# Linear attention before two feed-forward layers: attention by whole load groups, tail products over 128 rows, rms_g folded into the weights, the token scale on ScalarE

## The chip, the cores and the metric

One core of a Trainium2 chip. Its engines are named as in the profile: PE (TensorE matmuls; PEld is its weight load), DVE (VectorE), ACT (ScalarE), POOL (GpSimd) and SP (SyncE, which only issues DMAs). Each engine works through its own instructions in order. The metric is the device time of one execution in microseconds; lower is better.

## The reference

```python
def attn(q, k, v, omega):                 # 4 batches, 8 heads, 576 rows, D = 64, M = 128 features
    def phi(x):                           # x already scaled by D ** -0.25
        h = x @ omega.T - sum(x * x) / 2
        return exp(h - max(h)) / sqrt(M)
    kv, z = phi(k).T @ v, sum(phi(k))     # per batch and head
    return (phi(q) @ kv) / (phi(q) @ z + 1e-6)
def moe(x, w_gate, w_val, w_out, rms_g):  # 2304 tokens, 512 -> 1536 -> 512
    xn = x / sqrt(mean(x * x) + 1e-6) * rms_g
    return (silu(xn @ w_gate) * (xn @ w_val)) @ w_out
def moe2(x, w_in, w_out):                 # 512 -> 2048 -> 512
    return silu(x @ w_in) @ w_out
out = moe2(moe(tokens(attn(...))))        # inputs and weights come as float32 or float64
```

The weights come as float64 and are decoded on the chip. Every product with a weight is done in three passes (high by high, high by low, low by high).

## The kernel before, in words

**Attention and the first sweep.** The 576 rows of a batch are two halves of 256 rows and a tail of 64. One load (`add_load`) brings a half of four heads as a 128x512 tile; the tails of two batches share a tile of 128x256, the even batch in the first 64 partitions and the odd one in the last. A *unit* (`add_unit`) is half a load of a half, or a whole tail: 72 units, 36 of k and 36 of q. For each unit PE transposes 2 blocks (L586), ACT copies them out as the high part (L592), DVE subtracts for the low part (L595), PE does six 256-column products with omega (`pj`, L605), DVE takes the maxima (L620) and forms the bias in two small instructions (L626, L633) from the row norms (squared and halved on POOL, L545 and L549, ended on DVE, L558), and ACT does four exponentials (L644). A unit of k then adds its products with v into one PSUM bank (`kv`, L690); these have 128 rows and two output halves of 64 columns, while a tail of k has 64 rows and a full output. When a batch and four heads are done, DVE copies that bank out (`kvs`, L710). A unit of q is transposed on PE (L721), copied out by ACT (L727) and multiplied by kvs (L736, L742); DVE divides (L759 to L779).

When the heads of a half are complete, ACT squares and sums its tokens (L803), POOL makes rstd (L814, L817), DVE multiplies by rstd and rms_g (`xn`, L833), PE transposes (L842), and ACT and DVE write the high and low part of the tokens (L851, L856) into `xs`. There are 18 such tiles of 128 tokens in five blocks: four of 512 columns and one of 256.

**Weights.** A job (`w_load`, `w_decode`, `w_high`, `w_low`) loads 512 KB, decodes it with five DVE passes (L156 to L167) and two POOL passes (L170), and splits it on ACT (L180) and DVE (L183). Six jobs of the first sweep (two gates, two values, two outputs) and the first three of the second are put between the attention work (`add_weight`); each of the six waits for a numbered `pj`.

**Order.** All this, and the first sweep's products for blocks 0 to 2 (L236, L963), are `Op`s with a duration, dependences and buffer claims. `run_order` walks a model of the five engines and emits at each step the ready Op with the smallest `prio + RANK[kind]`; so the tables `RANK` and `SLOTS`, the durations and the Ops themselves set the order of every engine. Six PSUM banks (`b`) go round among transposes, projections and products.

**The stream.** After that the remaining products (blocks 3 and 4 of sweep 0, then ten more sweeps, five of them in all with gates and values) follow in a written order, and `Prep.tick` puts in a step of the weight pipe whenever PE has been given 3.2 us of work (until the second sweep's weights are in), later 5.5 us. The first product of the stream is the first `PE g L236`.

Of the kernel before, what the change touches and what calls it, by code (L numbers as in the profile page):

```python
# [20 lines left out]
def kernel(  # L21
# [68 lines left out]
    g_sb = const.tile([P, DM], F32)  # L90
# [60 lines left out]
    def w_decode(job, st, step, n=None):  # L151
# [36 lines left out]
    class Prep:  # L188
# [35 lines left out]
    W_EARLY, GRAIN = 3, 3  # L224
# [152 lines left out]
    class Op:  # L377
# [15 lines left out]
        "ld_om": 41.7, "t_om": -211.5, "s_om": -232.3, "bd_hi": -107.5, "bd_lo": 58.9,  # L393
# [4 lines left out]
        "rstd": -389.4, "xn": 36.2, "xf": -367.8, "x_hi": -48.8, "x_lo": 225.6, "ld_w": 11.5,  # L398
        "w_dec": 310.2, "w_add": 254.1, "w_hi": 67.9, "w_lo": 196.9, "part": 226.4, "tanh": 300.8,
        "silu": -31.9, "glu": 10.3, "h_hi": -176.1, "h_lo": -143.8, "out": 711.2, "ya": -190.5,  # L400
    }
    SLOTS = {
# [68 lines left out]
    small = ps_a.tile([P, SLOTS["nb"], 2 * G], F32, tag="small", name="small", bufs=1)  # L471
# [3 lines left out]
    def fetch(dst, src, kind, b, hf, g):  # L475
        heads = slice(G * g, G * g + G)
        if len(kind) == 2:
            for e in range(2):
# [18 lines left out]
    def k_units(b):  # L497
        for g in range(2):
            for hf in range(2):
                for hp in range(2 * g, 2 * g + 2):  # L500
                    yield "k", b, hf, hp, g
            if b % 2 == 0:
                yield "kt", b, 0, 0, g

    def q_units(b):
        for hf in range(2):
            for hp in range(4):
                yield "q", b, hf, hp, hp // 2
# [11 lines left out]
    last_use = {}  # L520
    for i, (kind, b, hf, hp, g) in enumerate(units):
        last_use[kind, b, hf, g] = i
    last_k = max(i for i, u in enumerate(units) if u[0][0] == "k")
# [5 lines left out]
    def add_load(u, i):  # L529
# [9 lines left out]
        w.op = Op("ld_x", "SP", 0.37 * R, emit, prio=i - 5, claim=["x"])  # L539
# [13 lines left out]
        w.sqop = Op("sq", "Pool", 0.26 + 0.43 * R, squares, [w.op], i - 1, ["sq", "ns"])  # L553
        h1 = Op("half1", "Pool", 0.25 + 0.28 * R, lambda o: halve(D // 2), [w.sqop], i - 2)
        h2 = Op("half2", "Pool", 0.26 + 0.14 * R, lambda o: halve(D // 4), [h1], i - 2)
# [6 lines left out]
        w.nsop = Op("norms", "DVE", 0.2, norms, [h2], i + 0.5, free=[(w.sqop, "sq")])  # L562
        if kind[0] == "k":
            z = vld[u] = State()

            def emit_v(o):
                z.v = va_tail[g] if tail else va_ring[o.slot["v"]]
                fetch(z.v, v, *u)

            z.op = Op("ld_v", "SP", 0.73 * R, emit_v, prio=i, claim=[f"vt{g}" if tail else "v"])  # L570

    def add_unit(i):
        kind, b, hf, hp, g = units[i]
        u = kind, b, hf, g
        tail = len(kind) == 2
        if u not in ld:
            add_load(u, i)
        w = ld[u]
        st = State()

        def transposes(o):
            st.pt = buf(ps_a, [P, 2, P], "b", o.slot["b"])
            st.hl = buf(wk, [P, 2, 2, P], "hl", o.slot["hl"], F32R)
            for j in range(2):
                h0, n = (2 * j, 2) if tail else (2 * (hp % 2) + j, 1)
                nc.tensor.transpose(  # L586
                    st.pt[:, j, :], w.x[:, h0:h0 + n, :, :].rearrange("p h r d -> p (h r d)"), ident
                )

        free_x = [(w.op, "x")] if last_use[u] == i else []  # L590
        tr = Op("tr", "PE", 0.218, transposes, [w.op, w.sqop], i - 1, ["b", "hl"], free_x)
        hi = Op("tr_hi", "ACT", 0.264, lambda o: nc.scalar.activation(out=st.hl[:, 0], in_=st.pt, func=AF.Copy), [tr], i - 0.3)  # L592
        lo = Op(
            "tr_lo", "DVE", 0.335,
            lambda o: nc.vector.tensor_tensor(  # L595
                out=st.hl[:, 1], in0=st.pt, in1=st.hl[:, 0].bitcast(F32), op=ALU.subtract
            ),
            [hi], i, free=[(tr, "b")],
        )

        def project(o):
            st.ps = buf(ps_a, [P, G, P], "b", o.slot["b"])
            for j in range(2):
                for n, (a, c) in enumerate(PASS):
                    nc.tensor.matmul(  # L605
# [478 lines left out]
```

## Time and profile before

| | us |
|---|---|
| median of 3 runs (1009.81 to 1011.66) | 1011.57 |
| the profiled execution's own time | 1011.63 |
| its span, first to last instruction | 1009.8 |
| PE busy in the span | 992.4 (98%) |
| first `PE g L236` of the stream | 218.18 |

The page gives for each engine the time in which an instruction ran on it. PE counts as busy while a matmul is in its pipe, and the ends of matmuls are modelled; so PE at 98% says that it nearly always had something in the pipe, not that it ran at its highest rate. The distance from the start of one group to the start of the next, where nothing is waited for, gives the rate. The other engines are read in the same way: the busy time of one instruction includes some latency that the next one overlaps.

### The profile page before, as it was taken

The page shows a single profiled execution, that of the slowest core. Times are in us where ns is not written, and L with a number is a line of the kernel's source. Part 1 is how long each engine was busy: PE and PEld are TensorE (multiplying, and loading weights), DVE is VectorE, ACT ScalarE, POOL GpSimd, SP SyncE. Part 2 cuts the span into 40 slices and gives each one's busy share as a digit, 9 for nine tenths or more (in the row PEclk, how much of TensorE's full clock was granted, in tenths as well). Part 3 has the DMA queues.
Part 4 walks back from the last instruction along what each step waited for, and adds up shares of the span by engine and source line. Part 5 has one row for each costly group of instructions (what it writes and reads, how often), then busy time and mean ns, then how long its engine had stood idle before and what let it go on. Part 6 is the DMA issues. An engine that isn't in the chain of part 4 may idle for free.

```text
span 1009.8 us, 15330 instructions
## 1 busy us (share of the span) xinstructions
PE 992.4 (98%) x5935; PEld 842.4 (83%) x5935; DVE 587.8 (58%) x1289; ACT 374.6 (37%) x861; POOL 282.2 (28%) x287
## 2 busy tenths in 40 slices
PE   7999998999999999999999999999999999999998
PEld 7988886788888888888888888888888888888887
DVE  7899998837852345676332776443654544535633
ACT  6988895344221112222111334433322322322321
POOL 6756632415520002344000231321411411201300
PEclk9999999999999999999999999999999999999999
DMA  7444211212320002222000120210210210200023
GB/s 196 123 122 131 67 30 42 64 41 84 104 63 1 1 1 64 63 85 83 21 1 1 42 63 22 84 42 5 79 42 6 78 42 22 63 1 21 21 84 105
DMA packets 68729, 55.85 MB, mean 55 GB/s; under 512 B 25648, under 2 KB 62768, under 8 KB 68656
## 3 DMA queue, kind: packets, MB, share of 16 engines
q1 hardware_dynamic: 68656, 54.87, 18.4%
q8 instruction: 47, 0.77, 0.3%
q14 instruction: 26, 0.21, 0.1%
HBM read 50.14 MB, written 4.72 MB: 54 GB/s over the span
## 4 chain that ended last, share of the span: by engine, by line
PE 89%; DVE 7%; issue 1%; POOL 1%; ACT 1%; DMA 1%; SPq 0%; DVEq 0%; ACTq 0%; POOLq 0%
PE g L236 43%; PE y L323 19%; PE y L290 12%; PE b L605 4%; PE b L236 3%; PE kv L690 2%; DVE small L620 2%; PE b L963 2%; PE b L736 1%; PE b L721 1%; PE b L586 1%; DVE hl L595 1%; DVE w L183 1%; POOL m L170 1%; DVE xt L833 1%
## 5 line engine op out<-in xcount | busy, mean ns | idle before, releaser
L236 PE MATMUL g<-xs,w 128*128 128x512 f32 (+1 forms) x2256 | 467.9, 366 | 0.0
L236 PEld LDWEIGHTS g<-xs,w 128*128 128x128 f32 x2256 | 391.2, 188 | 70.1
L170 POOL TENSOR_TENSOR m<-m,raw 128x512 int32<-128x512 int32 x136 | 189.9, 1396 | 612.6 <-issue 442.6
L230 DVE TENSOR_TENSOR h<-s,h 128x512 fp32r<-128x512 f32 (+1 forms) x134 | 96.0, 717 | 185.0 <-ACT h L229 185.0
L323 PE MATMUL y<-w,h 128*128 128x512 f32 (+1 forms) x870 | 200.8, 388 | 0.0
L323 PEld LDWEIGHTS y<-w,h 128*128 128x128 f32 x870 | 162.2, 188 | 33.3
L229 ACT ACTIVATE h<-s 128x512 fp32r<-128x512 f32 (+1 forms) x134 | 78.7, 588 | 191.5 <-DVE s L259 169.5
L290 PE MATMUL y<-h,w 128*128 128x512 f32 (+1 forms) x648 | 135.6, 366 | 0.3 <-DVE w L183 0.3
L290 PEld LDWEIGHTS y<-h,w 128*128 128x128 f32 x648 | 112.1, 189 | 20.5 <-DVE w L183 0.8
L270 ACT ACTIVATE s<-g 128x512 f32<-128x512 f32 (+1 forms) x80 | 44.4, 556 | 171.0 <-PE g L236 170.9
L334 DVE TENSOR_TENSOR ya<-y,ya 128x512 f32<-128x512 f32 (+1 forms) x91 | 62.2, 684 | 57.8 <-PE y L323 56.5
L259 DVE TENSOR_TENSOR s<-s,g 128x512 f32<-128x512 f32 (+1 forms) x54 | 33.8, 627 | 84.8 <-PE g L236 84.8
L301 DVE TENSOR_TENSOR ya<-y,ya 128x512 f32<-128x512 f32 (+1 forms) x80 | 50.2, 635 | 54.3 <-PE y L290 54.1
L180 ACT ACTIVATE w<-m 128x512 fp32r<-128x512 f32 x68 | 42.7, 628 | 102.8 <-POOL m L170 102.8
L644 ACT ACTIVATE e<-b,nb 128x128 f32<-128x128 f32 x272 | 77.5, 395 | 3.7 <-DVE nb L633 3.6
L605 PE MATMUL b<-bd,hl 128*128 128x256 f32 x432 | 69.5, 300 | 1.7 <-DVE hl L595 1.1
L605 PEld LDWEIGHTS b<-bd,hl 128*128 128x128 f32 x432 | 56.8, 192 | 5.4 <-DVE hl L595 2.3
L620 DVE TENSOR_REDUCE small<-b 128x4 f32<-128x512 f32 x72 | 50.2, 697 | 6.2 <-PE b L605 2.2
L253 ACT ACTIVATE s<-g 128x512 f32<-128x512 f32 (+1 forms) x54 | 29.7, 550 | 64.1 <-PE g L236 63.9
L183 DVE TENSOR_TENSOR w<-m,w 128x512 fp32r<-128x512 f32 x68 | 52.9, 779 | 0.1
L545 POOL TENSOR_TENSOR sq<-x 128x512 f32<-128x512 f32 (+1 forms) x40 | 38.9, 982 | 36.2 <-DMA x<-in_q_dram 9.8
L549 POOL TENSOR_TENSOR sq<-sq 128x256 f32<-128x256 f32 (+2 forms) x80 | 44.4, 573 | 2.3
(69 smaller groups left out, 739.7 us busy)
## 6 DMA issues: line engine op xcount, KB each, us to landing
raw<-in_moe_w_out_dram SPq DMA_DIRECT2D x28, 512.0 KB, 3.5
raw<-in_moe_w_in_dram SPq DMA_DIRECT2D x16, 512.0 KB, 3.7
raw<-in_moe_w_gate_dram SPq DMA_DIRECT2D x12, 512.0 KB, 3.6
raw<-in_moe_w_val_dram SPq DMA_DIRECT2D x12, 512.0 KB, 3.5
x<-in_k_dram SPq DMA_DIRECT2D x16, 256.0 KB, 3.4
va<-in_v_dram SPq DMA_DIRECT2D x32, 128.0 KB, 3.3
x<-in_q_dram SPq DMA_DIRECT2D x16, 256.0 KB, 3.0
out_dram<-ya SPq DMA_DIRECT2D x15, 256.0 KB, 2.0
```

The source lines that it names most:

```text
L170: tt(out=mi, in0=mi, in1=(low if step == 5 else high).bitcast(I32), op=ALU.add)
L183: nc.vector.tensor_tensor(out=st.t[:, 1, :], in0=st.m.bitcast(F32), in1=st.t[:, 0, :].bitcast(F32), op=ALU.subtract)
L229: nc.scalar.activation(out=ht[:, 0, :], in_=s, func=AF.Copy)
L230: nc.vector.tensor_tensor(out=ht[:, 1, :], in0=s, in1=ht[:, 0, :].bitcast(F32), op=ALU.subtract)
L236: nc.tensor.matmul(out=ps, lhsT=w[:, a, cc * P:(cc + 1) * P], rhs=xs[j][:, c, cc, :], start=(n == 0), stop=(n == 3 * KC - 1),)
L290: nc.tensor.matmul(out=ps, lhsT=wt[1, "o", f][:, a, d * P:(d + 1) * P], rhs=hs[f][:, c, :], start=(n == 0), stop=(n == nn - 1),)
L301: nc.vector.tensor_tensor(out=y[:, d, :], in0=ps, in1=y[:, d, :], op=ALU.add)
L323: nc.tensor.matmul(out=ps, lhsT=hs[f][:, a, t * P:(t + 1) * P], rhs=wt[2, "p", f][:, c, d0:d1], start=(n == 0), stop=(n == nn - 1),)
L334: nc.vector.tensor_tensor(out=o[:, t, d0:d1], in0=ps, in1=o[:, t, d0:d1], op=ALU.add)
L605: nc.tensor.matmul(out=st.ps[:, 2 * j:2 * j + 2, :].rearrange("p h m -> p (h m)"), lhsT=st.hl[:, c, j, :], rhs=bd[:, a, :], start=(n == 0) ...
L620: nc.vector.tensor_reduce(out=st.mx, in_=st.ps, axis=AX.X, op=ALU.max)
L644: nc.scalar.activation(out=st.e[:, h, :], in_=st.ps[:, h, :], func=AF.Exp, bias=st.nb[:, h:h + 1])
```

## The change

- A unit is now a whole load: one transpose group of four blocks, one high and one low copy of 128x512, then two projections, two maxima, one pair of the small bias instructions over 8 columns instead of 4, two groups of exponentials. A load of k ends in one `kv` group of 16 products.
- A tail's `v` tile is padded with zeros in the other batch's 64 partitions, and its products run over 128 rows with two output halves like the others. The tile is filled twice, once for each batch: POOL writes zeros and ones (`pad`), SP loads 64 rows (`ld_vt`). The second `pad` waits for the first batch's products.
- rms_g is loaded as 128x4 and multiplied into the gate and value weights by a third POOL pass (L173). The tokens are then scaled by rstd alone, on ACT (`xn`), and kvs is copied out by ACT as well. The sum of squares writes its unused output into `xs` instead of a buffer of its own.
- The first sweep's weight jobs wait for the `pj` of loads 3, 4, 5, ... instead of units 24, 26, 28, ...
- `RANK` has new values and separate ones for k and q, `SLOTS` has other counts (x 4, hl 2, e 4, nmc 2), several durations of the model are other, and `EDGE` is 72.

```diff
-        else:
+        elif step < 7:
             mi = st.m.bitcast(I32)
             tt(out=mi, in0=mi, in1=(low if step == 5 else high).bitcast(I32), op=ALU.add)
+        else:
+            mf = st.m.bitcast(F32).rearrange("p (c f) -> p c f", c=KC)
+            tt(out=mf, in0=mf, in1=g_sb.rearrange("p (c o) -> p c o", o=1).to_broadcast([P, KC, P]), op=ALU.mult)
+    def scaled(job):
+        return job[2][1] in "gv"
...
-                    for s in range(7):
+                    for s in range(8 if scaled(job) else 7):
...
-        "ev": -296.8, "num": -288, "den": -624.4, "rec": 84.2, "mu": 166, "ss": 2186.9,
+        "ev": -25.5, "num": -251.5, "den": 269.3, "rec": 818.1, "mu": 56.7, "ss": 1947.1,
...
+    def add_tail_v(u, i, e, prev):
+        kind, b, hf, g = u
+        t = va_tail[g]
+        def pad(o):
+            nc.gpsimd.memset(t[64 - 64 * e:P - 64 * e], 0.0)
+            nc.gpsimd.memset(t[64 * e:64 * e + 64, :, :, D:D + 1], 1.0)
+        po = Op("pad", "Pool", 0.35, pad, [prev], i - 2, [] if prev else [f"vt{g}"])
+        return po, Op("ld_vt", "SP", 0.36, lambda o: fetch(t, v, kind, b, hf, g, [e]), [po], i)
...
-            st.pt = buf(ps_a, [P, 2, P], "b", o.slot["b"])
-            st.hl = buf(wk, [P, 2, 2, P], "hl", o.slot["hl"], F32R)
+            st.pt = buf(ps_a, [P, 2 * R, P], "b", o.slot["b"])
+            st.hl = buf(wk, [P, 2, 4, P], "hl", o.slot["hl"], F32R)
+            for j in range(2 * R):
+                nc.tensor.transpose(st.pt[:, j, :], flat()[:, j * P:(j + 1) * P], ident)
...
+        for r in range(R):
+            def project(o, r=r):
...
-                    jobs.append((a, st.e[0:64, a, :], va.v[0:64, a, 0, :]))
+            return [(h, st.e[0][:, h, :], va_tail[g][:, h, 0, :]) for h in range(G)]
...
-                nc.vector.tensor_copy(out=acc.sb, in_=acc.ps)
+                nc.scalar.activation(out=acc.sb, in_=acc.ps, func=AF.Copy)
...
-            nc.vector.scalar_tensor_tensor(
-                out=st.x, in0=st.x, scalar=xs_.rstd[:, r:r + 1], in1=g_sb, op0=ALU.mult, op1=ALU.mult
-            )
-        xn = Op("xn", "DVE", 0.61, scale_x, [rs, g_op], i, free=[(xs_.sq[0], "rs")] if last else [], port=True)
+            nc.scalar.activation(out=st.x, in_=st.x, func=AF.Copy, scale=xs_.rstd[:, r:r + 1])
+        xn = Op("xn", "ACT", 0.53, scale_x, [rs], i, free=[(xs_.sq[0], "rs")] if last else [])
...
-            add_weight(job, n, [pj_ops[24 + 2 * n]])
+            add_weight(job, n, [pj_ops[GATE + n]])
```

How instructions move, in three places. In the names, b is a PSUM bank, hl the split transposes, e the exponentials, xt the tokens, w a weight of side and slot, xs the blocks of tokens; the number behind a name tells buffers apart.

PE before, from the last two projections (L605) to the first product of the stage with a weight (L236):

```order
L605 MATMUL b_3124<-bd,hl_3008 128x256 x6
L605 MATMUL b_3142<-bd,hl_3094 128x256 x6
L842 MATMUL b_3151<-ident,xt_2742 128x128 x4
L842 MATMUL b_3162<-ident,xt_2742 128x128 x4
L736 MATMUL b_3177<-kvs_2916,qT_3086 64x65 x8
L721 MATMUL b_3188<-ident,e_3137 128x128 x4
L721 MATMUL b_3199<-ident,e_3170 128x128 x4
L236 MATMUL b_3211<-xs_90,w_0_1833 128x512 x6
```

All of the stage's products with weights lie behind the last projection here. PE now, where the first such product (L242) stands between projections (L626) of the third batch and those of the second tail:

```order
L626 MATMUL b_1912<-bd,hl_1802 128x256 x6
L605 MATMUL b_1924<-ident,x_1696 128x128 x4
L242 MATMUL b_1935<-xs_90,w_0_1076 128x512 x3
L626 MATMUL b_1944<-bd,hl_1896 128x256 x6
L752 MATMUL b_1959<-ident,e_1930 128x128 x4
L626 MATMUL b_1966<-bd,hl_1896 128x256 x6
L626 MATMUL b_1978<-bd,hl_1925 128x256 x6
L626 MATMUL b_1988<-bd,hl_1925 128x256 x6
L878 MATMUL b_2006<-ident,xt_1365 128x128 x4
L242 MATMUL b_1935<-xs_90,w_0_1076 128x512 x9
```

All 48 products of block 0 with the four gate and value weights now stand ahead of the last projection; before, none of the stage's 144 did. 96 of them, and all 72 output products, still follow it.

ACT now, around the first tokens; L841 is the sum of squares, L871 the scaling that DVE did, L887 the high part of the tokens, L668 exponentials, L758 the copy of a transposed q:

```order
L841 ACTIVATE xs_90,ss_1080<-xt_725 128x4x128
L668 ACTIVATE e_1115<-b_1054,nb_1078 128x128 x4
L610 ACTIVATE hl_1121<-b_1120 128x512
L668 ACTIVATE e_1154<-b_1069,nb_1078 128x128 x4
L871 ACTIVATE xt_725<-xt_725,rstd_1081 128x512
L668 ACTIVATE e_1180<-b_1091,nb_1126 128x128 x4
L668 ACTIVATE e_1205<-b_1104,nb_1126 128x128 x4
L887 ACTIVATE xs_90<-b_1197 128x4x128
L758 ACTIVATE qT_1232<-b_1217 128x512
```

The scaling stands among the exponentials and waits for POOL's rstd; before, ACT had only L803 and L851 of these tokens in its row.

POOL now, at the start of the stream; m is a weight being decoded:

```order
L855 TENSOR_TENSOR rstd_3532<-ss_3531,mhalf 128x1
L170 TENSOR_TENSOR m_3626<-m_3626,raw_3592 128x512 x2
L173 TENSOR_TENSOR m_3626<-m_3626,g_sb 128x512
L170 TENSOR_TENSOR m_3695<-m_3695,raw_3635 128x512 x2
L173 TENSOR_TENSOR m_3695<-m_3695,g_sb 128x512
L170 TENSOR_TENSOR m_3733<-m_3733,raw_3704 128x512 x2
L173 TENSOR_TENSOR m_3733<-m_3733,g_sb 128x512
L170 TENSOR_TENSOR m_3780<-m_3780,raw_3742 128x512 x2
```

Each gate or value weight has a third pass; the three jobs of the second sweep that the stream prepares first are of that kind, and 24 of all 68 jobs.

## Rows read from the trace of the kernel before

**Rows 1.** The page: busy time and share of the span of each engine.
```profile
PE 992.4 (98%) x5935; PEld 842.4 (83%) x5935; DVE 587.8 (58%) x1289; ACT 374.6 (37%) x861; POOL 282.2 (28%) x287
```

**Rows 2.** Stretches: length, PE, PEld, DVE, ACT, POOL busy (instructions), granted clock, DMA.
```profile
0.00:158.00 158.00, 146.36 (x1822) 131.78 (x1823) 142.28 (x474) 133.21 (x434) 96.17 (x150) 0.99 0.41 107
158.00:218.18 60.18, 58.27 (x342) 46.65 (x341) 41.67 (x83) 27.21 (x53) 20.53 (x20) 0.99 0.20 62
25.00:150.00 125.00, 120.34 (x1569) 108.72 (x1567) 116.64 (x394) 111.00 (x363) 78.12 (x114) 1.00 0.36 96
155.00:158.00 3.00, 2.77 (x25) 2.65 (x26) 2.93 (x12) 2.09 (x8) 0.81 (x1) 0.58 0.00 0
264.32:1006.26 741.94, 741.92 (x3538) 625.02 (x3538) 371.06 (x677) 195.73 (x344) 145.36 (x104) 1.00 0.14 42
```

**Rows 3.** Chain of waits: start, length, engine, tile, line, count.
```profile
36.32 0.71 DVE small L620
37.06 0.16 DVE nb L633
...
42.13 0.71 PE b L605 x6
42.84 0.22 PE b L586 x2
43.06 0.44 PE b L721 x4
...
44.43 1.65 PE kv L690 x24
...
50.08 1.08 PE kv L690 x32
...
270.98 16.32 PE g L236 x72
```

**Rows 4.** Groups of DVE, 0 to 218.18 us: busy, mean ns, idle before.
```profile
L833 DVE SCALAR_TENSOR_TENSOR xt<-xt,rstd,g_sb 128x512 f32<-128x512 f32 x18 | 15.4, 879 | 1.8 <-POOL rstd L817 1.7
L710 DVE COPY kvs<-kv 128x260 f32<-128x260 f32 x8 | 3.4, 424 | 0.1
```

**Rows 5.** Timeline of ACT: start, length, line, operation, tiles, count.
```profile
28.75 0.45 ACT L592 ACTIVATE hl<-b 128x256 fp32r<-128x256 f32 x1
29.01 0.67 ACT L727 ACTIVATE qT<-b 128x512 f32<-128x512 f32 x1
29.49 2.26 ACT L644 ACTIVATE e<-b,nb 128x128 f32<-128x128 f32 x8
31.49 0.75 ACT L727 ACTIVATE qT<-b 128x512 f32<-128x512 f32 x1
...
140.09 0.66 ACT L803 ACTIVATE junk<-xt 128x512 bf16<-128x512 f32 x1
...
140.70 0.41 ACT L592 ACTIVATE hl<-b 128x256 fp32r<-128x256 f32 x1
...
145.09 0.66 ACT L180 ACTIVATE w<-m 128x512 fp32r<-128x512 f32 x1
145.61 1.35 ACT L851 ACTIVATE xs<-b 128x512 fp32r<-128x512 f32 x2
```

**Rows 6.** Timeline of POOL, with the idle time before and what ended it.
```profile
40.77 2.04 POOL L545 TENSOR_TENSOR sq<-x 128x512 f32<-128x512 f32 x2 [1.84 <-DVE ns L558]
...
239.65 2.69 POOL L170 TENSOR_TENSOR m<-m,raw 128x512 int32<-128x512 int32 x2 [1.42 <-ACT s L253]
```

**Rows 7.** Timelines of DVE and PE, at the second sweep's first output products.
```profile
244.94 0.68 DVE L183 TENSOR_TENSOR w<-m,w 128x512 fp32r<-128x512 f32 x1
...
256.96 1.79 DVE L183 TENSOR_TENSOR w<-m,w 128x512 fp32r<-128x512 f32 x1
...
264.32 6.66 PE L290 MATMUL y<-h,w 128*128 128x512 f32 x28 [0.33 <-DVE w L183]
```

**Rows 8.** Waits of ACT from 264 us on: us in total, times, longest.
```profile
ACT w L180 <- POOL m L170: 92.4, 21, 8.0
```

More of the change, by code (lines that the diff above doesn't have):

```diff
@@ L518 @@
             qs, ks = qs[1:], ks[1:]
[L520 to L523, printed above, removed]
+    place, at = [], 0
+    for u in units:
+        place.append(at)
+        at += 1 if len(u[0]) == 2 else 2
+    last_k = max(n for n, u in zip(place, units) if u[0][0] == "k")
     ld, vld, kvfirst, kvprev, kvcopy, ktexp, xtop = {}, {}, {}, {}, {}, {}, {}
@@ L599, in add_unit @@
         )
[L601 to L605, printed above, removed]
-                        out=st.ps[:, 2 * j:2 * j + 2, :].rearrange("p h m -> p (h m)"),
-                        lhsT=st.hl[:, c, j, :],
-                        rhs=bd[:, a, :],
-                        start=(n == 0),
-                        stop=(n == 2),
-                    )
@@ new lines, in add_unit, with maxima @@
+        for r in range(R):
+            def project(o, r=r):
+                st.ps[r] = buf(ps_a, [P, G, P], "b", o.slot["b"])
+                for j in range(2):
+                    for n, (a, c) in enumerate(PASS):
+                        nc.tensor.matmul(
+                            out=st.ps[r][:, 2 * j:2 * j + 2, :].rearrange("p h m -> p (h m)"),
+                            lhsT=st.hl[:, c, 2 * r + j, :],
+                            rhs=bd[:, a, :],
+                            start=(n == 0),
+                            stop=(n == 2),
+                        )
+            last = r == R - 1
+            pj = Op("pj." + kind[0], "PE", 0.715, project, [lo] + bd_ops, i, ["b", "pjc"], [(tr, "hl")] if last else [])
+            pjs.append(pj)
+            def maxima(o, r=r):
+                if r == 0:
+                    n = o.slot["nb"]
+                    st.mx, st.top = small[:, n, 0:G * R], small[:, n, 2 * G:2 * G + G * R]
+                    st.nb = buf(wk, [P, G * R], "nb", n)
+                nc.vector.tensor_reduce(out=st.mx[:, G * r:G * r + G], in_=st.ps[r], axis=AX.X, op=ALU.max)
+            mxs.append(Op("mx." + kind[0], "DVE", 0.64, maxima, [pj] + mxs, i, ["nb"] if r == 0 else []))
@@ L672, in add_kv, with add_products @@
+            num = None
+            for r in range(R):
+                num = add_q(u, i, st, r, evs, num)
+    def add_products(b, g, i, jobs, deps, first, end, dur, free):
         acc = kvfirst.setdefault((b, g), State())
@@ L709, in copy @@
                 acc.sb = buf(wk, [P, G, D + 1], "kvs", o.slot["kvs"])
-                nc.vector.tensor_copy(out=acc.sb, in_=acc.ps)
-            kvcopy[b, g] = Op("kvs", "DVE", 0.34, copy, [o], i, ["kvs"], [(acc.op, "kv")])
-    def add_q(i, st, ex):
-        kind, b, hf, hp, g = units[i]
-        tail = kind == "qt"
+                nc.scalar.activation(out=acc.sb, in_=acc.ps, func=AF.Copy)
+            kvcopy[b, g] = Op("kvs", "ACT", 0.31, copy, [o], i, ["kvs"], [(acc.op, "kv")])
+        return o
@@ new lines, in add_tail, with jobs, add_kv @@
+    def add_tail(b, g, e, i, st, ex, vop, pad, free):
+        def jobs():
+            return [(h, st.e[0][:, h, :], va_tail[g][:, h, 0, :]) for h in range(G)]
+        return add_products(b + e, g, i, jobs, [ex, vop], False, True, 0.47, free)
+    def add_kv(u, i, st, exs):
+        kind, b, hf, g = u
+        if kind == "kt":
+            pad, vop = add_tail_v(u, i, 0, None)
+            done = add_tail(b, g, 0, i, st, exs[0], vop, pad, [])
+            ktexp[b, g] = (u, st, exs[0], pad) + add_tail_v(u, i + 2, 1, done)
+            return
+        va = vld[u]
+        def jobs():
+            return [
+                (n // 2, st.e[n // G][:, n % G, :], va.v[:, n // 2, n % 2, :]) for n in range(2 * G)
+            ]
+        add_products(
+            b, g, i, jobs, exs + [va.op], hf == 0, False, 0.93, [(ex, "e") for ex in exs] + [(va.op, "v")]
+        )
+        if b % 2 and hf == 1:
+            tu, tst, tex, pad, _, vop = ktexp[b - 1, g]
+            add_tail(b - 1, g, 1, i, tst, tex, vop, pad, [(tex, f"et{g}"), (pad, f"vt{g}")])
@@ L727, in evac, with add_q @@
-            nc.scalar.activation(out=st.qt, in_=st.pe, func=AF.Copy)
-        ev = Op("ev", "ACT", 0.478, evac, [fl], i, ["qT"], [(fl, "b")])
+            st.e[r] = buf(wk, [P, G, P], "qT", o.slot["qT"])
+            nc.scalar.activation(out=st.e[r], in_=pe[0], func=AF.Copy)
+        return Op("ev", "ACT", 0.495, evac, [fl], i, ["qT"], [(fl, "b")])
+    def add_q(u, i, whole, half_unit, evs, prev):
+        kind, b, hf, g = u
+        tail = kind == "qt"
+        hp = 2 * g + half_unit
+        st = State()
+        ev = evs[half_unit]
@@ L876, in add_weight @@
             prev = Op(
[L877 removed]
+                "w_dec", "DVE", 0.37, lambda o, s=s: w_decode(job, st, s, o.slot.get("wm")), [lop, prev], pr,
                 [] if s else ["wm"], port=True,
```

228 lines of the change are left out of this document (100 added, 128 removed), and 7 rows, old and new, of tables (RANK, SLOTS).

## The prediction

> **What bounds the kernel now.** I read the page first, then the busy times by stretch, the chain of waits, and the timelines of PE and ACT where nothing is waited for. PE has something in its pipe for 98% of the span [rows 1], which by itself says only that the stages have to be looked at one by one. From 264.32 to 1006.26 us PE is busy for 741.92 of 741.94 us [rows 2], and 72 products of 512 columns take 16.32 us, 0.2267 us each [rows 3]: the stream runs at PE's rate and only fewer products or a new stall could move it; the change takes no product out of it. What can move is the time until the stream starts, 218.18 us in. I cut it at 158 us, where the first product with a weight stands.
>
> In the first 158 us three engines are near their limit: DVE busy 142.28, ACT 133.21, PE 146.36 [rows 2]. In the middle of it (25 to 150 us) DVE is at 116.64 of 125, 93%, ACT at 89% [rows 2]. PE's busy time deceives here; its work by rate is smaller. From the chain of waits [rows 3]: a projection of a unit 0.71, its two transposes 0.22, four transposes of exponentials or tokens 0.44, 32 kv instructions 1.08, so 0.54 for 16, and 24 of which 8 are a tail's 1.65, so 1.11 for the tail's 8. With the counts of the program: 72 x 0.93 = 67.0, 54 x 0.44 = 23.8, 32 kv and 36 numerators x 0.54 = 36.7, 8 tails x 1.11 = 8.9, 216 products with weights x 0.2267 = 49.0; together 185.4 us. Behind 158 us lie of it the 49.0 and 2 transposes, 6 numerators, 5 token flips, 55.3 in all, in 60.18 us: 4.9 lost. Ahead lie 130.1 in 158: 27.9 lost, 82% worked. The chain there runs again and again through DVE's maxima and small instructions [rows 3]. So the first stage is DVE's, with ACT close behind, and PE has nothing to fill its gaps, since every product with a weight comes later. One such gap lets the granted clock fall to a mean of 0.58 from 155 to 158 us [rows 2], partly the lower level of 1.2 GHz.
>
> **The change, part by part.**
> *Taken from DVE.* The scaling of 18 token tiles, 15.4 us, and 8 copies of kvs, 3.4 us [rows 4]. The pair of small instructions comes 40 times instead of 72: 64 fewer x 0.16 [rows 3] = 10.2 us. The subtraction of 512 columns for two of 256 I count as nothing. Of these 29.0 about two thirds of the scaling, all copies and all small pairs lie before 158 us: 24 of the 142.28. Were a quarter of the second stretch's 41.67 [rows 2] to come forward with block 0 and the weights, DVE would stand at some 128 us there. It is no longer first.
> *Put on ACT.* 18 scalings; nearest row, an ACT copy of 512 columns from SBUF, the start of the next 0.52 later [rows 5]: 9.4. Eight kvs copies at 0.26, the row for 256 columns: 2.1. The high copies become 32 x 0.48 + 8 x 0.26 for 72 x 0.26: less 1.3. Until the last exponential ACT then has 72 x 1.00 for exponentials (eight in 2.00), 17.4 high copies, 32 x 0.48 transposed q, 15 x 0.61 sums of squares, 13 scalings 6.8, 13 x 0.48 tokens, kvs 2.1, six weights 3.1, block 0 about 2: 134 us [rows 5]. The scaling waits for POOL's rstd and exponentials stand behind it; DVE waited 1.7 us in all for the same thing [rows 4], and I leave it at that.
> *Taken from PE.* A tail's products have the form of the others: 8 x (1.11 - 0.54) = 4.6. PE's work until the stream is 180.8.
> *Moved on PE.* 48 of the 144 products with weights now stand between attention work. Behind the last projection remain 168 x 0.2267 = 38.1 and the same 6.3 of other things: 44.4. Ahead: 136.4.
> *Added on POOL and SP.* Eight pads, each two small fills, and seven third passes in the stage. A float multiply of this shape takes 1.02 (two in 2.04), the integer pass 1.35 [rows 6]; those are the bounds, and I take 1.02, the same operation. Together some 10 us on an engine busy for 96.17 of 158 [rows 2]: hidden. The second pad of a tail waits for PE's products of the even batch; behind it on POOL stand squares and halvings, thus norms and exponentials, and on SP, behind `ld_vt`, the next x and v loads. Those loads run several units ahead. I count nothing, at worst 1 us for each of 4.
> *Earlier weights.* Two gates are fetched beside the first q and k loads. A gap of the DMA queue there would cost a few us at the start and is in the range.
> *Sum.* PE with 136.4 and ACT with 134 are now level and first. The engine that bounded before was busy for 142.28 of 158, 90%, the empty start included [rows 2]. At that share the last projection comes at 136.4 / 0.90 = 151.5 us. With 44.4 and the 4.9 lost as now the stream starts at 200.8 instead of 218.2: 17.4 us gained. At 95% and 2 lost it is 190.0 (28.2 gained), at 85% 209.8 (8.4).
> *Lost in the stream.* At 264.32 PE waits 0.33 us for the last of the second sweep's weights [rows 7], so that pipe has no slack, and three of its six jobs get a third POOL pass. The passes of the first two fall partly into POOL's idle time (1.42 before the pass at 239.65 [rows 6]), the third delays what follows: 1.0, between 0 and 3 x 1.35 = 4.1.
> 1011.63 (the profiled execution, 0.06 over the median) - 17.4 + 1.0 = 995.2; I say 995.
>
> *The port.* A weight's low part on DVE takes 0.68 us alone and 1.79 while POOL runs a decoding pass [rows 7]. The Trainium skill (SBUF — State Buffer, Who interferes with whom) says that a DVE instruction with two SBUF inputs and a POOL instruction that reads SBUF exclude each other for the whole of one. The rows agree; by it a third pass can block DVE for a whole pass more in each scaled job, which is the mechanism of the slower rival below.
>
> **The rivals.**
> *ACT takes DVE's place.* Every wait on POOL or PE now falls into a full ACT queue. If ACT gets no better share than now, 133.21 of 158, 84% [rows 2], its 134 end at 159 us and the stream starts at 208.3: 9.9 gained, 1002.7. For it: ACT is already at 89% in the middle. Against: it is the follower there, not the bound. The Trainium skill (ScalarE: Activation LUTs, Rules for kernel authors) says to put multiplies on VectorE, not on ScalarE, which speaks for this case; the rows here give 0.52 on ACT against a mean of 0.879 on DVE [rows 4, 5], so for a DVE that shares its port they differ.
> *PE nearly full.* With weights ready early there is always something to issue: 190.0, the 95% case, 984.4. For it: the products need only block 0 and one gate. Against: they stand at fixed places in the order, and six banks are shared by all.
> *The order does not hold on the chip.* The rows of each engine are fixed by a model; if its gaps stay, PE works 82% as now: 136.4 / 0.823 + 49.3 = 215.0, and 1009.4.
> *Slower: the third pass reaches PE.* Of the 24 scaled jobs 17 are in the stream. ACT's copy of a weight waits for POOL already, 92.4 us in 21 waits [rows 8], with silu and the high parts behind it and PE's banks behind these. If each job cost PE a whole pass, 17 x 1.35 = 23 us, the time would be 1017; it decides from 1.0 us per job on. Against: those 92.4 us cost PE 0.02 us in 742 [rows 2].
>
> **How the numbers follow.** Forecast 0.57 (its own range 989 to 1001), ACT the bound 0.19, PE nearly full 0.13, order not holding 0.05, slower 0.06. The range of 984 to 1006 leaves out most of the last two and the faster half of the nearly full case. A measurement of this kernel tells 0.2%, 2 us, from no change. Faster: 0.57 + 0.19 + 0.13 and a little of the fourth, 0.90; the rest of the fourth is the same, 0.04; slower 0.06.
>
> **What would show it.** The first stream product near 201 us; a last projection near 151; DVE in the middle of the attention below 88% and ACT or PE at 90% or more; the tail's kv group at about half its length; 48 products with weights before the last projection at 0.23 us each; PE's wait for the second sweep's outputs between 0.3 and 4 us; PE full from there on. I am wrong if the stream starts after 210 us, if PE has gaps behind it at each scaled weight, or if ACT's waits for rstd add up to more than 5 us.

## The result, and the profile after

The changed kernel takes 998.32 us (998.12 to 998.77), the kernel before 1010.93: ratio 0.9877, 95% interval 0.986 to 0.9894. The prediction said 995.0, with 984 to 1006. The profiled execution took 998.12 us, 13.5 less than the one of before, with a span of 996.0. The one of before ran at a mean granted clock of 0.998; beside the runs below, 20 executions of that kernel at 0.998 took 1011.3 in the median and 20 at 1.000 took 1009.7, so some 1.6 us of the 13.5 belong to a fall of the clock that half of its executions do not have.

Stretches of the changed kernel, with the columns of [rows 2]; the first ends with the last projection, the second with the first product of the stream:

```profile
0.00:156.77 156.77, 145.02 (x1934) 133.98 (x1935) 137.77 (x376) 141.44 (x427) 112.30 (x175) 1.00 0.45 118
156.77:202.90 46.13, 45.96 (x294) 37.08 (x293) 24.20 (x58) 26.09 (x54) 14.57 (x15) 1.00 0.13 40
25.00:150.00 125.00, 120.12 (x1683) 111.67 (x1679) 115.86 (x319) 120.32 (x367) 91.51 (x134) 1.00 0.41 106
155.00:158.00 3.00, 3.00 (x22) 2.74 (x21) 2.86 (x8) 2.78 (x8) 0.14 (x1) 1.00 0.56 175
250.00:992.50 742.50, 742.05 (x3538) 625.05 (x3538) 377.75 (x679) 196.59 (x344) 161.96 (x118) 1.00 0.13 42
```

In the middle of the attention (the third row) PE and ACT stand at 96% and DVE at 93%, where before PE had 96% too, DVE 93% and ACT 89% [rows 2]. The stretch from 155 to 158 us, at a granted clock of 0.58 before, is at 1.00. The stream is as full as it was.

The chain of waits of the changed kernel (start, length, engine, tile, line, count), at the last projection, the first stream product and 72 products of the stream:

```profile
155.32 1.46 PE b L626 x12
156.77 2.75 PE b L242 x12
...
202.90 9.34 PE g L242 x41
256.99 16.32 PE g L242 x72
```

The stream starts 15.3 us earlier than before (218.18) and products run at the same 16.32 for 72 [rows 3]. From there to the end of the span it takes 996.0 - 202.90 = 793.1 us, before 1009.8 - 218.18 = 791.6: 1.5 lost. So 15.3 - 1.5 = 13.8 is the whole difference of the spans.

PE's timeline, at the last tail's products and at the only wait of over 0.15 us in the stream:

```profile
136.87 1.15 PE L694 MATMUL kv<-va,e 128*64 128x65 f32 x32
137.85 0.64 PE L694 MATMUL kv<-vat,et 128*64 128x65 f32 x16
138.32 0.87 PE L777 MATMUL b<-kvs,qT 128*64 128x65 f32 x24
...
250.35 6.64 PE L296 MATMUL y<-h,w 128*128 128x512 f32 x28 [1.20 <-DVE w L189]
```

A tail's 16 products now take 0.47 us (137.85 to 138.32), where 8 took 1.11 before. The wait for the second sweep's weight is 1.20, 0.33 before [rows 7].

Groups of ACT, DVE and POOL until the stream starts (busy us, mean ns, idle before):

```profile
L871 ACT ACTIVATE xt<-xt,rstd 128x512 f32<-128x512 f32 x18 | 13.2, 766 | 0.0
L714 ACT ACTIVATE kvs<-kv 128x260 f32<-128x260 f32 x8 | 3.6, 453 | 0.1
```

```profile
L614 DVE TENSOR_TENSOR hl<-b,hl 128x512 fp32r<-128x512 f32 (+1 forms) x40 | 25.2, 631 | 2.8 <-ACT hl L610 2.1
L189 DVE TENSOR_TENSOR w<-m,w 128x512 fp32r<-128x512 f32 x9 | 7.2, 803 | 0.2 <-ACT w L186 0.2
L649 DVE SCALAR_TENSOR_TENSOR small<-ns,small 128x8 f32<-128x8 f32 (+1 forms) x40 | 6.6, 165 | 0.6
L656 DVE SCALAR_TENSOR_TENSOR nb<-ns,small 128x8 f32<-128x8 f32 (+1 forms) x40 | 6.1, 155 | 0.6
```

```profile
L173 POOL TENSOR_TENSOR m<-m,g_sb 128x512 f32<-128x512 f32 x7 | 7.9, 1126 | 0.2
L587 POOL MEMSET vat<- 64x260 f32 x8 | 2.5, 308 | 5.3 <-PE kv L694 3.6 <-POOL m L173 0.9 <-POOL m L170 0.5
```

The scaling on ACT never waited for rstd (idle 0.0). The subtraction (L614), which the prediction counted as nothing, takes 25.2 us where it took 29.4. The pads waited 3.6 us for PE's products, and nobody behind them shows it: after the first 6 us and until the stream starts the only engine seen waiting for POOL is ACT, 2.7 us for a third pass.

### The profile page after: what moved, and what is told of

Its sections match the earlier page's. It is cut to its first block, busy times and chain, and to the rows that moved or that the text cites. A ratio compares the mean times of both kernels' runs of the same rounds, so it can differ in the third digit from the quotient of the medians.

```text
span 996.0 us, 15344 instructions
## 1 busy us (share of the span) xinstructions
PE 979.2 (98%) x5999; PEld 835.1 (84%) x5999; DVE 575.9 (58%) x1167; ACT 381.0 (38%) x855; POOL 312.7 (31%) x325
## 4 chain that ended last, share of the span: by engine, by line
PE 89%; DVE 5%; ACT 3%; issue 1%; DMA 0%; SPq 0%; DVEq 0%; ACTq 0%
PE g L242 44%; PE y L329 20%; PE y L296 12%; PE b L626 4%; PE b L242 3%; PE b L999 2%; ACT e L668 2%; PE kv L694 1%; PE b L752 1%; PE b L777 1%; DVE small L643 1%; PE b L605 1%; DVE w L189 1%; PE b L878 1%; DVE m L156 1%
## 5 line engine op out<-in xcount | busy, mean ns | idle before, releaser
L242 PE MATMUL g<-xs,w 128*128 128x512 f32 (+1 forms) x2256 | 468.0, 366 | 0.0
L242 PEld LDWEIGHTS g<-xs,w 128*128 128x128 f32 x2256 | 391.1, 188 | 70.0
L170 POOL TENSOR_TENSOR m<-m,raw 128x512 int32<-128x512 int32 x136 | 190.5, 1401 | 562.3 <-issue 421.4
L236 DVE TENSOR_TENSOR h<-s,h 128x512 fp32r<-128x512 f32 (+1 forms) x134 | 96.9, 724 | 185.1 <-ACT h L235 185.1
L235 ACT ACTIVATE h<-s 128x512 fp32r<-128x512 f32 (+1 forms) x134 | 78.7, 588 | 183.3 <-DVE s L265 161.3
L276 ACT ACTIVATE s<-g 128x512 f32<-128x512 f32 (+1 forms) x80 | 44.4, 556 | 171.0 <-PE g L242 170.9
L186 ACT ACTIVATE w<-m 128x512 fp32r<-128x512 f32 x68 | 42.9, 631 | 116.4 <-POOL m L170 69.0
L668 ACT ACTIVATE e<-b,nb 128x128 f32<-128x128 f32 x272 | 78.5, 418 | 4.7 <-DVE nb L656 4.0
L626 PE MATMUL b<-bd,hl 128*128 128x256 f32 x432 | 65.2, 295 | 2.8 <-DVE hl L614 1.8
L626 PEld LDWEIGHTS b<-bd,hl 128*128 128x128 f32 x432 | 56.3, 193 | 5.9 <-DVE hl L614 2.5
L189 DVE TENSOR_TENSOR w<-m,w 128x512 fp32r<-128x512 f32 x68 | 55.6, 817 | 0.2 <-ACT w L186 0.2
```

Of the source, the lines that this page charges most:

```text
L189: nc.vector.tensor_tensor(out=st.t[:, 1, :], in0=st.m.bitcast(F32), in1=st.t[:, 0, :].bitcast(F32), op=ALU.subtract)
L235: nc.scalar.activation(out=ht[:, 0, :], in_=s, func=AF.Copy)
L236: nc.vector.tensor_tensor(out=ht[:, 1, :], in0=s, in1=ht[:, 0, :].bitcast(F32), op=ALU.subtract)
L242: nc.tensor.matmul(out=ps, lhsT=w[:, a, cc * P:(cc + 1) * P], rhs=xs[j][:, c, cc, :], start=(n == 0), stop=(n == 3 * KC - 1),)
L626: nc.tensor.matmul(out=st.ps[r][:, 2 * j:2 * j + 2, :].rearrange("p h m -> p (h m)"), lhsT=st.hl[:, c, 2 * r + j, :], rhs=bd[:, a, :], sta ...
L668: nc.scalar.activation(out=st.e[r][:, h, :], in_=st.ps[r][:, h, :], func=AF.Exp, bias=st.nb[:, G * r + h:G * r + h + 1],)
```

## The experiments

The theory that the prediction rests on (A): the change takes work from VectorE, which set the first stage's end. Its rivals: the early products with weights fill TensorE's waits (B); the refitted order does it (C); the tails' shorter products do it. All times are medians; "later" is against the changed kernel's 998.32, and the stream's start against 202.90. The kernel before, measured again beside each group of runs, gave medians of 1009.64 to 1011.15, so a "later" of 1 to 2 us is not told from nothing by the times alone; the last two columns are of one execution each.

| run | us | later | ratio to before, interval | stream from | stream lasts |
|---|---|---|---|---|---|
| tails over 64 rows | 1003.47 | 5.2 | 0.9925 to 0.9951 | 207.97 | 793.4 |
| no third pass in the stream | 996.85 | -1.5 | 0.986 to 0.9885 | 203.61 | 791.7 |
| scaling on DVE, order kept | 1005.87 | 7.6 | 0.9951 to 0.9975 | 210.60 | 793.2 |
| the same, old form | 1015.27 | 17.0 | 1.005 to 1.0074 | 214.96 | 797.8 |
| late products with weights | 1002.50 | 4.2 | 0.9904 to 0.9934 | 207.25 | 792.9 |
| old ranks | 1001.08 | 2.8 | 0.9891 to 0.9921 | 206.78 | 793.1 |
| ACT + 18 copies | 1007.79 | 9.5 | 0.9966 to 0.9986 | 213.20 | 793.1 |
| DVE + 18 maxima | 1018.45 | 20.1 | 1.0063 to 1.0092 | 224.76 | 793.0 |
| omega early, weights faster | 1008.39 | 10.1 | 0.996 to 0.9983 | 202.48 | 804.0 |
| scaling on DVE, planned | 999.61 | 1.3 | 0.9872 to 0.9903 | 204.68 | 793.0 |
| before, one-operand scaling | 1008.00 | 9.7 | 0.9964 to 0.9982 | 214.24 | 791.4 |
| omega early, weights sooner | 1001.30 | 3.0 | 0.9894 to 0.9921 | 202.30 | 797.3 |

**Tails over 64 rows.**

```diff
-                for c in HALVES:
+                for c in HALVES if lhsT.shape[0] == P else [slice(0, P)]:
...
-            return [(h, st.e[0][:, h, :], va_tail[g][:, h, 0, :]) for h in range(G)]
+            return [(h, st.e[0][64 * e:64 * e + 64, h, :], va_tail[g][64 * e:64 * e + 64, h, 0, :]) for h in range(G)]
```

> The changed kernel with one part undone: the tails of both sweeps multiply over 64 rows with full output, as before the change, in the same order of instructions. That puts 4.6 us of TensorE work back ahead of the last projection (the tail group of 16 products took 1.11 us for 8 before, .54 for 16 now). If TensorE sets the stage's end (it is busy 120.1 of 125 us in 25 to 150), the stream starts 3.5 to 4.6 us later: 1002 to 1003. If ScalarE sets it (120.3 of 125), part of that hides in TensorE's waits: 0.5 to 2 us, 999 to 1000.5. If VectorE still sets it, nothing: 998.3.

Measured 5.2 us later. The stretch to its last projection, by engine as above:

```profile
0.00:161.87 161.87, 150.46 (x1870) 138.83 (x1871) 137.29 (x376) 141.78 (x427) 111.99 (x175) 1.00 0.44 114
```

5.1 us more than 156.77 for the same ACT and DVE work and 4.6 of TensorE's by the prediction's rows (the tail groups of this run take 1.03 us each from start to start against 0.47, 4.5 in all). So in this order TensorE's work counts in full in this stage. The 0.5 us more, just beyond the expected range, is no more than executions of one kernel differ by (998.12 to 998.77).

**No third pass in the stream.**

```diff
-                    for s in range(8 if scaled(job) else 7):
+                    for s in range(7):
```

> The changed kernel, but the 17 weight jobs that run beside the stream leave out GpSimd's third pass, the multiplication by rms_g (so rms_g is missing from those weights). The theory that the third pass costs the stream only at its start, where TensorE waited 1.2 us for a weight from VectorE: 997 to 997.3. A rival, that it costs the stream nothing and the 1.2 us is the late start of the chain of weights: 998.3. A second rival, that each of the 17 passes slows VectorE's decoding through the shared port by its own 1.04 to 1.38 us and this reaches TensorE more than once: 990 or less.

This run leaves rms_g out of the stream's weights. Measured 1.5 us less, which the times alone do not tell from nothing; but the stream lasts 791.7 us, as long as before the change, and PE's wait shrinks to the old size:

```profile
249.79 6.65 PE L296 MATMUL y<-h,w 128*128 128x512 f32 x28 [0.34 <-DVE w L189]
```

The first theory holds: the third pass costs the stream 1.4 us, 1.3 of it before the end of the second sweep's first output products (202.90 to 256.99 us against 203.61 to 256.44), and next to nothing after it.

**Scaling on DVE, order kept**, and **the same in the old form.**

```diff
-            nc.scalar.activation(out=st.x, in_=st.x, func=AF.Copy, scale=xs_.rstd[:, r:r + 1])
+            nc.vector.tensor_scalar(out=st.x, in0=st.x, scalar1=xs_.rstd[:, r:r + 1], scalar2=None, op0=ALU.mult)
```

```diff
+    ones = const.tile([P, 1], F32)
...
-            nc.scalar.activation(out=st.x, in_=st.x, func=AF.Copy, scale=xs_.rstd[:, r:r + 1])
+            nc.vector.scalar_tensor_tensor(
+                out=st.x, in0=st.x, scalar=xs_.rstd[:, r:r + 1], in1=ones.to_broadcast([P, DM]), op0=ALU.mult, op1=ALU.mult
+            )
```

> The changed kernel with the 18 token scalings by rstd moved from ScalarE to VectorE, as one multiplication by a per-row scalar, everything else in the same order. ScalarE loses 11.0 us (18 at .61 from start to start), VectorE gains 18 instructions of .35 to .88 us, 6 to 16 us. Theory A, VectorE was the bound and still is nearly one (115.9 of 125 us in 25 to 150): the stream starts 4 to 10 us later, 1002 to 1008. Rival, ScalarE is now the bound (120.3 of 125) and VectorE has room: the same or up to 4 us earlier, 994 to 998.5.

> As the run before it, but with VectorE's two-operand form that the kernel before used (mean .879 us, with the shared port among its causes). VectorE gains 15.8 us, ScalarE loses 11.0. Theory A (VectorE is what the change relieved): the stream starts 9 to 14 us later, 1007 to 1012, that is most of the gain gone. Rival (the gain comes from the early weight products and the refitted order): at most 4 us later, 998 to 1002. Against the run before it: the form of the instruction itself is worth 3 to 9 us, if VectorE is the bound.

The stream starts 7.7 and 12.1 us later, within the ranges of theory A; the second run's time, 1015.27, lies beyond its range by what follows. The scaling's group on DVE in the first and in the second run:

```profile
L871 DVE TENSOR_SCALAR xt<-xt,rstd 128x512 f32<-128x512 f32 x18 | 12.9, 720 | 1.7 <-POOL rstd L855 1.7
```

```profile
L872 DVE SCALAR_TENSOR_TENSOR xt<-xt,rstd,ones 128x512 f32<-128x512 f32 x18 | 17.6, 984 | 1.7 <-POOL rstd L856 1.7
```

The form is worth 4.7 us of DVE and 4.4 of the start. The old form's run loses a further 4.7 in the stream, which is not the scaling's: some of its sweeps run 36 products in 8.39 us instead of 8.16 at a full granted clock. That run has one small constant tile more; whether the weights' place does it was not tried.

**Late products with weights.**

```diff
-    W_EARLY, GRAIN, GATE = 3, 3, 3
+    W_EARLY, GRAIN, GATE = 3, 3, 13
```

> The changed kernel with its weight products held back: the planner lets the first of the 144 products that merge the weights start only near the end of the projections, where the kernel before had them, so that some 36 of the 48 now ahead of the last projection go behind it (36 x .23 = 8.3 us of TensorE). Theory B, these products fill waits of TensorE: the last projection ends as now (156.8) or 1 to 3 us earlier, the stretch behind it grows by 8.3, and the stream starts 5 to 8 us later, 1003 to 1006. Rival, TensorE sets the stage's end all through: they only change places, 998 to 999.5.

The edit makes the six weight jobs of the first sweep wait for projections ten loads later, and their products with them. Measured 4.2 later: 1002.50 lies between the two expectations, just under B's 1003 to 1006. Until the last projection (149.43 + 1.42 = 150.85) only 12 products with weights are left, against 48 in the changed kernel (this run first, then the changed kernel; each count holds one product of the next group):

```profile
L242 PE MATMUL b<-xs,w 128*128 128x512 f32 x13 | 3.6, 400 | 0.0
```

```profile
L242 PE MATMUL b<-xs,w 128*128 128x512 f32 x49 | 14.7, 413 | 0.0
```

36 products are 8.2 us of TensorE. Ahead of the last projection they cost 156.77 - 150.85 = 5.9; behind it they added (207.25 - 150.85) - 46.13 = 10.3. So 2.3 us of the 8.2 fell into waits ahead, and 2.1 us of waits went behind. The last projection came 5.9 us earlier, not 0 to 3. With the products some work on their weights went behind it too: DVE is busy there for 31.68 us, against 24.20 in the changed kernel. So the 4.2 us is the price of late products and late weights together; the products alone were not tried.

**Old ranks.**

```diff
-        "ev": -25.5, "num": -251.5, "den": 269.3, "rec": 818.1, "mu": 56.7, "ss": 1947.1,
...
+        "ev": -296.8,
+        "num": -288,
...
```

> The changed kernel with the table of ranks that the kernel before had, so that the order of the first stage is planned anew from the old numbers. Theory C, the refitted order carries a good part of the gain: 1002 to 1008. Rival, the work that each engine does carries it, and the order only follows: 998 to 1001.

Measured 2.8 later, between the two: the fitted numbers of this table carry about a fifth of the gain, the other edits together the rest. `SLOTS`, `EDGE` and the durations of the model stayed as changed, so the work by itself is not what the rest measures.

**ACT + 18 copies, DVE + 18 maxima.**

```diff
             nc.scalar.activation(out=st.x, in_=st.x, func=AF.Copy, scale=xs_.rstd[:, r:r + 1])
+            nc.scalar.activation(out=st.x, in_=st.x, func=AF.Copy)
```

```diff
             nc.scalar.activation(out=st.x, in_=st.x, func=AF.Copy, scale=xs_.rstd[:, r:r + 1])
+            nc.vector.tensor_tensor(out=st.x, in0=st.x, in1=st.x, op=ALU.max)
```

> The changed kernel with an extra copy in place on ScalarE behind each of the 18 token scalings, the same order otherwise: 18 x .52 = 9.4 us more on ScalarE. If ScalarE is now the engine that sets the stage's end: 6.5 to 9.5 us later, 1005 to 1008. If VectorE is: 0 to 3 us, 998 to 1001 (the tokens come later by .52 each, which the prefetch of the next group should cover). If TensorE is: about 2 to 4 us, 1000 to 1002.

> The changed kernel with an extra operation on VectorE in place behind each of the 18 token scalings (the maximum of the tile with itself), the same order otherwise: 18 x .6 to .9 = 11 to 16 us more on VectorE. If VectorE still sets the stage's end: 9 to 15 us later, 1007 to 1013. If ScalarE does: VectorE has some 9 of 125 us free, so 2 to 7 us, 1000 to 1005.

9.5 later for 9.4 us of ACT: the upper end of "ScalarE sets it", though a part is TensorE's clock: in 75 to 100 us of that run it is granted at 0.86, worth up to 0.14 x 25 = 3.5 us (columns as above):

```profile
75.00:100.00 25.00, 21.73 (x259) 20.21 (x258) 19.80 (x59) 22.45 (x69) 14.71 (x26) 0.86 0.33 85
```

20.1 later for the maxima, beyond either theory. Their group:

```profile
L872 DVE TENSOR_TENSOR xt<-xt 128x512 f32<-128x512 f32 x18 | 14.9, 834 | 9.9 <-ACT xt L871 9.8
```

14.9 us of work and 9.9 in which DVE stood waiting for ACT's scaling, which the order had not foreseen. This run measures a wait in the wrong place as much as DVE's load, and by itself it is no evidence for A.

**Scaling on DVE, planned.** The kept order leaves the same doubt on the two runs with the scaling on DVE, so the planner was told.

```diff
-            nc.scalar.activation(out=st.x, in_=st.x, func=AF.Copy, scale=xs_.rstd[:, r:r + 1])
+            nc.vector.tensor_scalar(out=st.x, in0=st.x, scalar1=xs_.rstd[:, r:r + 1], scalar2=None, op0=ALU.mult)
...
-        xn = Op("xn", "ACT", 0.53, scale_x, [rs], i, free=[(xs_.sq[0], "rs")] if last else [])
+        xn = Op("xn", "DVE", 0.45, scale_x, [rs], i, free=[(xs_.sq[0], "rs")] if last else [])
```

> The token scalings on VectorE as one multiplication by a per-row scalar, as in the run that cost 7.5 us, but the planner is told of it (VectorE, .45 us) and orders the first stage anew. If those 7.5 us are VectorE's added work (18 x .57 = 10 us, of which ScalarE's relief gives nothing back): 1004 to 1007 again. If they are the old order's, whose rows on VectorE wait where ScalarE's did not: 997 to 1001, since the sum of the work of the three engines changes little (VectorE +10, ScalarE -11).

999.61: 6.3 of the 7.6 us were the order's, and 5.9 of the 7.7 at the stream's start. Under the kept order PE waited for the scaling, between 25 and 150 us of that run:

```profile
PE b L878 <- DVE xt L871: 3.3, 4, 1.7
```

In the planned run no engine is seen to wait for it. The group is also shorter with the same form: three of its 18 instructions take over 0.6 us, each beside a POOL pass, where under the kept order it was nine, each beside one too:

```profile
L871 DVE TENSOR_SCALAR xt<-xt,rstd 128x512 f32<-128x512 f32 x18 | 10.1, 573 | 0.4 <-POOL rstd L855 0.2
```

Theory A in its simple form (VectorE must lose the scaling) falls here: with an order made for it, the scaling may stay on DVE for 1.3 us, 0.13% and less than can be told from nothing, with the form of one operand tile. The old form with an order of its own was not tried.

**Before, one-operand scaling.**

```diff
-            nc.vector.scalar_tensor_tensor(
-                out=st.x, in0=st.x, scalar=xs_.rstd[:, r:r + 1], in1=g_sb, op0=ALU.mult, op1=ALU.mult
-            )
+            nc.vector.tensor_scalar(out=st.x, in0=st.x, scalar1=xs_.rstd[:, r:r + 1], scalar2=None, op0=ALU.mult)
```

> The kernel before, with its token scaling on VectorE in the form with one operand tile: rms_g is left out of the computation, everything else and the order are as they were. That is what folding rms_g into the weights allows by itself: 18 x (.879 - .57) = 5.6 us less of VectorE, 13 of the 18 in the first 158 us. If VectorE's busy time set the first stage's end, as the prediction had it: 4 to 5.5 us earlier, 1005.5 to 1007. If the order's fixed waits set it, 0 to 2 us: 1009 to 1011.

This run leaves rms_g out. 2.6 us less than before (1010.62 beside it), between the two expectations; beside those of the accompanying executions of the kernel before whose granted clock was 1.000 (1009.87 in the median; 0.999 to 1.000 in this run) it is 1.9. The group went from 15.4 us [rows 4] to:

```profile
L833 DVE TENSOR_SCALAR xt<-xt,rstd 128x512 f32<-128x512 f32 x18 | 10.4, 601 | 1.8 <-POOL rstd L817 1.7
```

5.0 us off DVE gave 2 to 2.6: under its order, even in the kernel before, DVE alone did not set the end.

**Omega early, weights faster**, and an attempt at a faster version, **omega early, weights sooner.**

```diff
-    W_PACE, W_RUSH = 5.5, 3.2
+    W_PACE, W_RUSH = 5.5, 2.4
...
-            lambda o: nc.sync.dma_start(
+            lambda o: nc.scalar.dma_start(
```

```diff
-        due = 0.0
+        due = 2.0
...
-            lambda o: nc.sync.dma_start(
+            lambda o: nc.scalar.dma_start(
```

> The changed kernel with two edits at the two places where TensorE waits outside the attention. Omega is fetched by ScalarE's queue as its first instruction instead of third on SyncE's, since its landing at 5.17 us ended TensorE's first wait (4.01 before the change); and the weights of the stream's first sweeps are prepared at 2.4 instead of 3.2 us of stream work, so that the one wait of the stream (1.2 us at 250.35 for a weight of VectorE) goes. If a shift at the start is carried to the end, because no engine has slack (extra work on each engine cost about its own length in the runs so far), the stream starts 1 to 2 us earlier; if the order absorbs it in later waits, 0. The stream gains 1.2, or loses if twice the rate of passes blocks VectorE. Together 995 to 996 if both hold, 997 if only the second does, 998.3 if none, above that if the rate of passes hurts.

> An attempt at a faster version: the changed kernel with omega fetched by ScalarE's queue (the run with it began the stream .4 us earlier), and the weight jobs of the stream each begun one piece of PE work (2.6 us) earlier but at the old rate, so that the second sweep's last weights are there when TensorE asks. If the 1.2 us wait at 250.35 is only lateness, it goes: 996.5 to 997. If any shift of these jobs puts ScalarE's copies, which wait for GpSimd's passes, ahead of the high parts that TensorE waits for (7.2 us at the doubled rate): 1000 to 1008.

The early omega brings the stream's start forward by 0.4 and 0.6 us. Both ways of hurrying the weights lose more than that. PE and then ACT in the first of the two runs:

```profile
231.10 0.51 PE L296 MATMUL y<-h,w 128*128 128x256 f32 x3
237.27 5.09 PE L296 MATMUL y<-h,w 128*128 128x256 f32 x21 [5.65 <-ACT h L235]
```

```profile
231.90 0.63 ACT L186 ACTIVATE w<-m 128x512 fp32r<-128x512 f32 x1 [3.95 <-POOL m L170]
232.43 0.37 ACT L259 ACTIVATE s<-g 128x256 f32<-128x256 f32 x1
236.28 0.63 ACT L186 ACTIVATE w<-m 128x512 fp32r<-128x512 f32 x1 [3.48 <-POOL m L170]
236.82 0.40 ACT L235 ACTIVATE h<-s 128x256 fp32r<-128x256 f32 x1
```

The high part that PE waits for (L235) stands in ACT's row behind a copy of a weight (L186), which waits for POOL's pass. That is the path of the prediction's slower rival, brought on by the pace of the jobs; the pass waited for here is one of the two that every weight has (L170), not the third. The two stretches, the wait and what follows it:

```profile
230.00:237.20 7.20, 1.62 (x9) 1.22 (x7) 4.09 (x7) 1.82 (x5) 4.66 (x4) 0.98 0.23 73
237.27:242.36 5.09, 5.09 (x22) 4.92 (x23) 1.01 (x2) 1.58 (x4) 0.00 (x0) 0.50 0.33 103
```

PE was busy for 1.62 of 7.20 us, and then ran at a granted clock of 0.50, the lower level of 1.2 GHz. The second run, with the old pace, shows the same in small: a wait of 2.48 us at 229.92 for L235, and 0.53 from 232 to 237 us. It beats the kernel before, not the changed one; no run that computes the whole reference did.

## Why the prediction was right, and where it was off

- *The stream can only start earlier.* Right: 15.3 us at its start, 1.5 lost behind it, every other us in its place.
- *PE at 136.4 us of work ahead of the last projection, at a share of 90%.* The work came as counted: 48 products with weights, 13 token flips, tails at less than half length (4.6 us; undoing them cost 5.1 there). The share was 136.4 / 156.77 = 87%, so the last projection came at 156.8 instead of 151.5. This is the term that was mis-sized most, by 5.3 us. It held 82% before, and I gave it the share that DVE had had by its busy time; no row supported carrying that over to PE.
- *Behind it 44.4 of work and 4.9 lost.* 46.13, so 1.7 lost. This made good 3.2 of the 5.3. Holding the products and their weights back put 2.1 us of waits there again. So the start of the stream, 2.1 us from the forecast, is in part luck: two errors of opposite sign.
- *DVE is no longer first.* The sum of the removed work was about right, the conclusion not: 93% in the middle, where I wanted to see below 88%, and 137.77 us ahead of the last projection, where I had some 128. Until the stream the durations of DVE's instructions add up to some 30 us less, but its busy time fell from 142.28 + 41.67 to 137.77 + 24.20, by 22.0, since its instructions overlap; and 17.5 us of the second stretch came forward where I moved 10.4. The undoing runs show the consequence: under the kept order PE and ACT have no room. 4.6 us of PE cost 5.2, 9.4 of ACT cost 9.5, the fall of the clock included. For DVE no run shows it, since the one with more DVE work is spoiled by a wait.
- *ACT at 134.* 141.44 busy until the last projection. Part of the difference is that the 134 adds distances from start to start, and busy time is longer: the same sum for the kernel before gives some 121, where 133.21 were busy. Two terms were too small: a scaling starts its follower 0.61 later (below), not 0.52, and a kvs copy, of 260 columns, is busy for 0.45, not 0.26; together 2.7 at most. The rival that gave ACT 84% ended the projections at 159, and 156.8 is nearer to that than to 151.5: in the prediction's own terms 134 / 156.77 is 85%. It missed the stream's start (208.3) by the stretch behind. But ACT alone is not the bound either: the planned run takes 18 x 0.61 = 11.0 us from it and gains nothing.

```profile
82.40 0.71 ACT L871 ACTIVATE xt<-xt,rstd 128x512 f32<-128x512 f32 x1
83.01 0.59 ACT L758 ACTIVATE qT<-b 128x512 f32<-128x512 f32 x1
```

- *Whether the scaling belongs on ACT.* The rows of before gave 0.879 on DVE against 0.52 on ACT, and I took the difference for the engine's. It is the form's and the order's: with one operand tile and a planned order DVE needs 0.573. By the Trainium skill (ScalarE: Activation LUTs, Rules for kernel authors) multiplies go on VectorE; the pair of runs puts the two engines 1.3 us apart, within 0.2%. So these runs neither bear the page out nor speak against it: beside a DVE that is about as full as ACT, and with the order made anew, the place hardly matters.
- *The third pass costs the stream 1.0 (0 to 4.1).* 1.4 to 1.5, and none later. The Trainium skill (SBUF — State Buffer, Who interferes with whom) says that a DVE instruction with two SBUF inputs and a GpSimd instruction that reads SBUF contend for a port pair that only one of them holds at a time. The trace agrees: the low part of the last weight took 1.77 us beside a POOL pass (below). That is not what the third pass adds, since without it the same instruction took 1.80; through which earlier one the 0.9 us more of PE's wait come was not followed. That each scaled job would cost PE a pass (1017) did not come; at the old pace the wait stays with ACT.

```profile
246.74 3.00 POOL L170 TENSOR_TENSOR m<-m,raw 128x512 int32<-128x512 int32 x2 [2.48 <-issue]
248.53 1.77 DVE L189 TENSOR_TENSOR w<-m,w 128x512 fp32r<-128x512 f32 x1
```

- *What was left out.* PE's first instruction waits for omega until 5.17 us, 4.01 before; an earlier fetch gave 0.4 to 0.6 us at the stream's start. The granted clock's return in 155 to 158 us is worth (1.00 - 0.58) x 3 = 1.3 us, which the sum had inside its 90%.

Of the 12.6 us, undoing one part at a time takes away 5.2 (tails), 4.2 (early weights and products) and 2.8 (ranks); these need not add up, since an undoing can also leave an order that fits less well. What the units of a whole load, the other `SLOTS` and the kvs copies on ACT do by themselves was not tried, so how much of the gain is theirs stays open.

## What to carry to other kernels

When three engines stand within a few per cent of each other, name the order as a bound of its own: here one operation moved to another engine cost 6 us more under the kept order than with the order made anew, and only the second says what the work is worth. Before an operation is moved to another engine, look whether its form is what makes it dear: in the kernel before, dropping one operand tile took 5.0 us off DVE and 2 to 2.6 off the time, while the move with an order of its own was not told from nothing. And a share of busy time belongs to its engine: it cannot be given to the next bound.

## What the runs showed of the hardware

- A multiplication of 128x512 by a per-row scalar on DVE took 0.455 us at the least and 1.264 at the most in one run, and 0.573 or 0.720 in the mean of two orders. Where no POOL instruction ran beside it, it took 0.455 to 0.486 in both runs; each of the 12 that took over 0.6 stood beside one.
- After a wait of PE of 5.65 us the granted clock was 0.50 for the next 5.09 us, so by an estimate from these two numbers that wait cost 0.50 x 5.09 = 2.5 us more than its length; after the wait of 1.20 us in the changed kernel it stayed at 1.00.
- In one run products of 512 columns took 0.233 us instead of 0.2267 in some sweeps, at a full granted clock; the cause is open:

```profile
764.20 8.39 PE g L243 x36
772.59 8.17 PE y L330 x36
780.76 8.39 PE g L243 x36
789.15 8.17 PE y L330 x36
```
